# Fourier mixing and a gated feed-forward layer on one core: a row loaded 11 steps ahead, and a sigmoid written into PSUM

## The chip, the core and the metric

The kernel runs on one core of a Trainium2 chip. The metric is the device time of one execution in microseconds, as the median of several runs. The names of the engines are those of the profile: PE is TensorE's matmul, PEld its weight load, DVE is VectorE, ACT ScalarE, POOL GpSimd, and SP is SyncE, which here only issues transfers.

## The reference

The input x has 8 sequences of S = 3008 rows with 256 features. A Fourier transform runs over the rows and then over the features, and the real part is kept. Each row of the result then goes through a gated layer with 1536 hidden features, all in fp32:

```python
X = np.fft.fft(x, axis=1)
X = np.fft.fft(X, axis=2)
x = X.real.reshape(B * S, D)
gate = 1.0 / (1.0 + np.exp(-(x @ w_gate)))
val = x @ w_val
out = (gate * val) @ w_out
```

## The kernel before, in words

**Work.** The kernel uses the symmetry of a real transform. For one sequence it computes two tables, pk and qk, over k = 0 to 1504. Row k of the transform is their sum, and row S-k is their difference. So one pass over k gives the hidden features of two rows, k and S-k, and the matmuls are done once for both. The feature transform is merged into the gate and value weights ahead of the loop (G1 and G2).

**Loop.** A sequence is cut into 6 chunks of up to 252 values of k, and a chunk into 12 steps, one for each block of 128 hidden features. This makes 576 steps. A step i belongs to group p = i // 3. The profile calls the buffers of a step by name: pf is one PSUM bank with two halves, gate in `pf[:, 0]` and value in `pf[:, 1]`. Three banks take turns for pf. The helper `mm` at line 134 issues every matmul, so all of PE's rows carry L134, and the tile tells which they are.

The life of a step is spread over its neighbours:

- `seed(i)` (line 595, two ACT instructions, run in step i-1; none for the first 12 steps) fills the bank with row E, the contribution of the middle feature. E comes in a tile ek that one transfer broadcasts to 128 partitions for a whole chunk (line 583, in `e_rows`).
- `front_a(i)` (PE, pf<-pk) adds the pk part. `part(i)` (line 611, ACT) then copies twice the bank into the tile ae.
- `front_b(i)` (PE, pf<-qk) adds the qk part, after which the bank holds gate and value of rows k. It must come after the copy of line 611.
- `gate_a(i)`, in step i+1: ACT writes the sigmoid of the gate half to the tile h (line 630), and DVE subtracts the bank from ae into the tile z, gate and value of rows S-k (line 635; line 632 in a few early steps).
- `gate_b(i)`, in step i+1: DVE multiplies h by the value half of the bank (line 647), ACT takes the sigmoid of `z[:, 0]` (line 648), and DVE multiplies it by `z[:, 1]` into the other half of h (line 649). POOL then forms sums of blocks of h in the tile sf (line 655).
- `back(p, part)` (PE, po<-h,wf and po<-sf,wf, five matmuls in a step, ten records in the trace) multiplies by the output weights. This is a fast bilinear scheme, so at the end of each chunk DVE has 20 additions in the tile c (line 719) and some transposes and copies (lines 729 and 696) to do. They are put on a list, of which two or three are taken in each of the following steps.

**Order.** Every engine runs its instructions in the order written. In step i ACT runs line 630 for step i-1, 611 for i, 595 twice for i+1, and 648 for i-1; DVE runs 635, 647 and 649 for i-1 and then what it takes from the list. What is done beside the steps hangs on step numbers (`at(i, f)`): the mirrored copy of the next sequence in DRAM (lines 160 to 169), its load into x (line 148), folds of x on POOL (lines 388 to 417) and DVE (line 428), and the row E. The transfers of line 583 go through SP's queue, behind whatever SP was given before. Two buffers take turns for ek.

The whole transform of a later sequence (tiles ev and od) is computed in the midst of the steps, once per sequence.

Of the kernel before, what the change touches and what calls it, by code (L numbers as in the profile page):

```python
# [10 lines left out]
AF = mybir.ActivationFunctionType  # L11
ALU = mybir.AluOpType
# [69 lines left out]
def kernel(  # L82
# [10 lines left out]
    nc = tc.nc  # L93
# [35 lines left out]
    op = ctx.enter_context(tc.tile_pool(name="op", bufs=1))  # L129
# [440 lines left out]
    H, SF, EK = {}, {}, {}  # L570

    def cut(i):
        b, c, _ = groups[i // 3]
        k0, n = chunks[c]
        f = i % NFT
        return PQE[b], slice(k0, k0 + n), n, f, slice(f * P, (f + 1) * P)

    def e_rows(i):

        b, c, _ = groups[i // 3]  # L580
        k0, n = chunks[c]
        EK[i // NFT] = ekp.tile([P, CH], F32, name="ek", tag="ek")[:, 0:n]
        nc.sync.dma_start(out=EK[i // NFT], in_=ed[b : b + 1, k0 : k0 + n].to_broadcast([P, n]))

    PF, AP, Z = {}, {}, {}
# [51 lines left out]
    def block(p, i):  # L637

        R = 2 * chunks[groups[p][1]][1] // 3
        return H[p][:, i % 3, i // 3 * R : (i // 3 + 1) * R] if i < 9 else SF[p][:, i - 9, 0:R]  # L640

    def gate_b(i):

        n = cut(i)[2]
        p, fh = i // 3, i % 3
        z, h = Z.pop(i), H[p]
        nc.vector.tensor_tensor(h[:, fh, 0:n], h[:, fh, 0:n], PF.pop(i)[:, 1], op=ALU.mult)  # L647
        nc.scalar.activation(z[:, 0], z[:, 0], AF.Sigmoid)  # L648
        nc.vector.tensor_tensor(h[:, fh, n:], z[:, 0], z[:, 1], op=ALU.mult)  # L649
        if p < NG:  # L650
            return
        if fh == 1:
            SF[p] = sp.tile([P, 8, 2 * CH // 3], F32, name="sf", tag="sf")
        for dst, a, b, op in H_SUMS.get(fh, ()):
            nc.gpsimd.tensor_tensor(block(p, dst), block(p, a), block(p, b),  # L655
                                    op=(ALU.subtract, ALU.add)[op])
# [174 lines left out]
    def at(i, *fs):  # L831
        side.setdefault(i, []).extend(fs)
# [17 lines left out]
    i0 = NFT  # L850
# [12 lines left out]
    at(3 * i0 + 6, table_again)  # L863
    at(4 * i0 + 5, lambda: [at(4 * i0 + 6 + i, f) for i, f in enumerate(table_odd())])
    for i in range(i0, count, i0):
        at(i - 8, lambda i=i: e_rows(i))

    for b in range(B - 1):
        s0 = b * per
# [21 lines left out]
    for i in range(count):  # L891
        front_a(i)
        if N1 <= i < NFT:
            part(i)
        if i:
            gate_a(i - 1)
        if not N1 <= i < NFT:
            part(i)
        if i0 <= i + 1 < count:
            seed(i + 1)  # L900
        if i:
            gate_b(i - 1)
        for f in pre.pop(i, []) + use.pop(i, []):
            f()
        if i >= 5:
            back((i - 5) // 3, (i - 5) % 3)
        front_b(i)
        n = 3 if i >= count - 8 else 2 + i % 2
        for f in later[0:n]:
            f()  # L910
        del later[0:n]
        for f in side.pop(i, []):
            f()
    gate_a(count - 1)
    gate_b(count - 1)
    for f in later:
        f()
# [51 lines left out]
```

## Time and profile before

| | |
|---|---|
| Time, median of 3 runs | 1952.96 us (1952.14 to 1953.48) |
| The profiled execution's own time, and its span | 1955.09 us, 1953.3 us |
| Mean granted clock of TensorE | 0.995 |
| Busy: PE, PEld, DVE, ACT, POOL | 1919.4, 1781.1, 1587.8, 1330.9, 1611.4 us |
| Chain that ended last, by engine | PE 89%, DVE 4%, POOL 4%, ACT 1%, DMA 1% |
| Transfer ek<-ed (line 583) | 47 of them, 126 KB or 123 KB each |

The span is the time from the first to the last instruction. The chain that ended last is followed back from the last instruction, at each link to what released it. A wait "A <- B: 3.9, 7, 1.4" reads: A sat idle until B, 3.9 us in total, 7 times, 1.4 us the longest. In a timeline a row has its start, its length, the engine, line, operation, tiles and count, and in brackets the idle time before it and what ended it. Matmuls overlap each other in the record, so starts tell PE's pace better than lengths.

### The profile page before, as it was taken

The page shows a single profiled execution, that of the slowest core. Times are in us where ns is not written, and L with a number is a line of the kernel's source. Part 1 is how long each engine was busy: PE and PEld are TensorE (multiplying, and loading weights), DVE is VectorE, ACT ScalarE, POOL GpSimd, SP SyncE. Part 2 cuts the span into 40 slices and gives each one's busy share as a digit, 9 for nine tenths or more (in the row PEclk, how much of TensorE's full clock was granted, in tenths as well). Part 3 has the DMA queues.
Part 4 walks back from the last instruction along what each step waited for, and adds up shares of the span by engine and source line. Part 5 has one row for each costly group of instructions (what it writes and reads, how often), then busy time and mean ns, then how long its engine had stood idle before and what let it go on. Part 6 is the DMA issues. An engine that isn't in the chain of part 4 may idle for free.

```text
span 1953.3 us, 34335 instructions
## 1 busy us (share of the span) xinstructions
PE 1919.4 (98%) x11180; PEld 1781.1 (91%) x11180; DVE 1587.8 (81%) x3250; ACT 1330.9 (68%) x3120; POOL 1611.4 (82%) x2802
## 2 busy tenths in 40 slices
PE   6999999999999999999999999999999999999997
PEld 4779889999999999999999999999999999999997
DVE  6677898997888978888878887788788887777777
ACT  3566657666777677776777767777677766777775
POOL 3269998997999888997889979998799986777776
PEclk8999999999999999999999999999999999999999
DMA  8342413112012120212013121211210110011011
GB/s 270 104 129 16 115 36 103 46 24 83 14 47 57 16 79 14 57 49 78 15 25 79 17 79 25 47 49 21 83 17 14 22 20 14 14 22 19 15 19 27
DMA packets 171978, 96.78 MB, mean 50 GB/s; under 512 B 136090, under 2 KB 163868, under 8 KB 169252
## 3 DMA queue, kind: packets, MB, share of 16 engines
q1 hardware_dynamic: 169842, 94.06, 20.3%
q8 instruction: 90, 1.47, 0.3%
q10 hardware_dynamic: 1926, 0.52, 0.1%
q14 instruction: 88, 0.72, 0.1%
q0 software_dynamic: 32, 0.00, 0.0%
HBM read 69.83 MB, written 46.71 MB: 60 GB/s over the span
## 4 chain that ended last, share of the span: by engine, by line
PE 89%; DVE 4%; POOL 4%; ACT 1%; DMA 1%; SPq 0%; issue 0%; DVEq 0%; POOLq 0%; ACTq 0%
PE pf L134 46%; PE po L134 38%; PE ev L134 3%; POOL sf L655 2%; DVE c L719 2%; PE od L134 1%; DVE h L649 1%; PE ps L134 1%; DMA x<-in_xf_dram 1%; DVE z L635 1%; ACT z L648 1%; POOL x L401 0%; ACT pf L595 0%; DMA ek<-ed 0%; SPq L740 0%
## 5 line engine op out<-in xcount | busy, mean ns | idle before, releaser
L655 POOL TENSOR_TENSOR sf<-h 128x168 f32<-128x168 f32 (+1 forms) x940 | 539.7, 592 | 203.9 <-DVE h L649 203.8
L655 POOL TENSOR_TENSOR sf<-h,sf 128x168 f32<-128x168 f32 (+1 forms) x1128 | 645.1, 591 | 44.2 <-DVE h L649 44.2
L134 PE MATMUL pf<-qk,G 128*128 128x252 f32 (+1 forms) x2304 | 583.1, 376 | 4.0 <-ACT ae L611 3.9
L134 PE MATMUL pf<-pk,G 128*128 128x252 f32 (+1 forms) x2304 | 583.9, 376 | 2.3 <-ACT pf L595 2.3
L649 DVE TENSOR_TENSOR h<-z 128x252 f32<-128x252 f32 (+1 forms) x576 | 316.5, 549 | 301.3 <-ACT z L648 300.8
L595 ACT ACTIVATE pf<-ek,ge 128x252 f32<-128x252 f32 (+1 forms) x1128 | 531.6, 471 | 21.3 <-DMA ek<-ed 2.9
L134 PE MATMUL po<-sf,wf 128*128 128x168 f32 (+1 forms) x3008 | 519.8, 306 | 0.2
L719 DVE TENSOR_TENSOR c<-c 128x168 f32<-128x168 f32 (+1 forms) x929 | 505.7, 575 | 5.4 <-ACT c L696 0.3
L134 PEld LDWEIGHTS pf<-pk,G 128*128 128x128 f32 x2304 | 436.0, 190 | 56.4 <-ACT pf L595 3.4
L611 ACT ACTIVATE ae<-pf 128x504 f32<-128x504 f32 (+1 forms) x569 | 334.7, 588 | 217.3 <-PE pf L134 215.5
L134 PEld LDWEIGHTS po<-sf,wf 128*128 128x128 f32 x3008 | 463.4, 190 | 9.0 <-POOL sf L655 0.9
L134 PE MATMUL po<-h,wf 128*128 128x168 f32 (+2 forms) x2640 | 469.9, 307 | 0.0
L134 PEld LDWEIGHTS pf<-qk,G 128*128 128x128 f32 x2304 | 410.3, 190 | 37.6 <-ACT ae L611 6.7
L134 PEld LDWEIGHTS po<-h,wf 128*128 128x128 f32 x2640 | 420.7, 190 | 17.3 <-issue 0.9
L635 DVE TENSOR_TENSOR z<-ae,pf 128x504 f32<-128x504 f32 (+1 forms) x569 | 377.6, 664 | 16.2 <-ACT h L630 15.6
L648 ACT ACTIVATE z<-z 128x252 f32<-128x252 f32 (+1 forms) x576 | 232.7, 404 | 162.5 <-DVE z L635 147.5
L630 ACT ACTIVATE h<-pf 128x252 f32<-128x252 f32 (+1 forms) x576 | 216.4, 376 | 126.2 <-PE pf L134 118.9
L647 DVE TENSOR_TENSOR h<-h,pf 128x252 f32<-128x252 f32 (+1 forms) x576 | 232.1, 403 | 0.0
L655 POOL TENSOR_TENSOR sf<-sf 128x168 f32<-128x168 f32 (+1 forms) x188 | 108.6, 577 | 14.7
L655 POOL TENSOR_TENSOR sf<-sf,h 128x168 f32<-128x168 f32 (+1 forms) x188 | 106.8, 568 | 0.0
L134 PE MATMUL ev<-st,x 63*128 63x189 f32 (+3 forms) x372 | 73.6, 348 | 7.3 <-DVE x L398 7.1
L696 ACT COPY c<-po 128x504 f32<-128x504 f32 (+1 forms) x141 | 78.4, 556 | 3.1 <-PE po L134 3.1
(141 smaller groups left out, 898.9 us busy)
## 6 DMA issues: line engine op xcount, KB each, us to landing
x<-xr SPq DMA_DIRECT2D x14, 1536.0 KB
out_dram<-os SPq DMA_DIRECT2D x372, 56.0 KB
xr<-in_xf_dram SPq DMA_DIRECT2D x14, 768.0 KB
xr<-in_xf_dram SPq DMA_DIRECT2D x35, 256.0 KB
ek<-ed SPq DMA_DIRECT2D x39, 126.0 KB
out_dram<-os SPq DMA_DIRECT2D x284, 7.0 KB
st<-in_stab_dram SPq DMA_DIRECT2D x4, 1111.9 KB
x<-in_xf_dram SPq DMA_DIRECT2D x2, 1512.0 KB
```

Source lines behind the costliest of these rows:

```text
L134: nc.tensor.matmul(o, l, r, start=start, stop=stop, skip_group_check=True)
L595: nc.scalar.activation(PF[i][:, g], EK[i // NFT], AF.Copy, scale=ge[:, g, f : f + 1])
L611: nc.scalar.activation(AP[i], PF[i], AF.Copy, scale=2.0)
L630: nc.scalar.activation(H[p][:, fh, 0:n], PF[i][:, 0], AF.Sigmoid)
L635: nc.vector.tensor_tensor(z[:, :, ::-1], AP.pop(i), PF[i], op=ALU.subtract)
L647: nc.vector.tensor_tensor(h[:, fh, 0:n], h[:, fh, 0:n], PF.pop(i)[:, 1], op=ALU.mult)
L648: nc.scalar.activation(z[:, 0], z[:, 0], AF.Sigmoid)
L649: nc.vector.tensor_tensor(h[:, fh, n:], z[:, 0], z[:, 1], op=ALU.mult)
L655: nc.gpsimd.tensor_tensor(block(p, dst), block(p, a), block(p, b), op=(ALU.subtract, ALU.add)[op])
L696: (nc.vector.tensor_copy if t == 1 or t == 3 and not last else nc.scalar.copy)(C[0][:, 3 * t * R : 3 * (t + 1) * R], PO[t][:, 0 : 3 * R])
L719: engine.tensor_tensor(t[:, dst * R : (dst + 1) * R], *v, op=(ALU.subtract, ALU.add)[op])
```

## The change

Two edits that do not touch each other's lines.

The first is to `gate_b`. The bank of a step is kept until the end of it. The sigmoid of line 648 still reads `z[:, 0]`, but writes to `pf[:, 0]`, the gate half of the step's bank, which has been read by then. The multiply of line 649 reads it from there, so that one of its inputs lies in PSUM and one in SBUF. `z[:, 0]` is no longer written over.

The second is to the place of `e_rows`: the row E of a chunk is loaded 11 steps before the chunk's first step, where it was 8 steps. The first chunk that uses it (i = i0 = 12) keeps 8.

```diff
         p, fh = i // 3, i % 3
-        z, h = Z.pop(i), H[p]
-        nc.vector.tensor_tensor(h[:, fh, 0:n], h[:, fh, 0:n], PF.pop(i)[:, 1], op=ALU.mult)
-        nc.scalar.activation(z[:, 0], z[:, 0], AF.Sigmoid)
-        nc.vector.tensor_tensor(h[:, fh, n:], z[:, 0], z[:, 1], op=ALU.mult)
+        z, h, pf = Z.pop(i), H[p], PF.pop(i)
+        nc.vector.tensor_tensor(h[:, fh, 0:n], h[:, fh, 0:n], pf[:, 1], op=ALU.mult)
+        nc.scalar.activation(pf[:, 0], z[:, 0], AF.Sigmoid)
+        nc.vector.tensor_tensor(h[:, fh, n:], pf[:, 0], z[:, 1], op=ALU.mult)
...
     for i in range(i0, count, i0):
-        at(i - 8, lambda i=i: e_rows(i))
+        at(i - (8 if i == i0 else 11), lambda i=i: e_rows(i))
```

In the built program the number and order of the instructions on PE, DVE, ACT and POOL stay as they were. On SP the transfer of the second chunk's row now stands ahead of the two loads of x (line 148), and that of some later chunks ahead of a mirror transfer. Three kinds of waits are new targets of old instructions: the sigmoid of line 648 waits for the multiply of line 647 of its own step (before, for line 635), and the seed of line 595 and, in the first chunk, the first matmul into a bank wait for the multiply of line 649 of the step that had the bank (before, line 647).

## Prediction

> **What bounds the kernel now.** I asked four things in this order: is PE ever idle, who makes it wait, what does one such wait look like, and what do the touched instructions cost. First the table of busy time by stage (columns: stretch, its length, busy time of PE, PEld, DVE, ACT, POOL with counts, then clock and DMA):
>
> ```profile
> 140.00:150.00 10.00, 7.72 (x34) 6.78 (x34) 2.23 (x6) 3.88 (x10) 4.39 (x10) 0.83 0.44 40
> ...
> 160.00:320.00 160.00, 157.24 (x953) 143.53 (x953) 139.91 (x275) 104.38 (x251) 147.11 (x252) 1.00 0.27 69
> 320.00:480.00 160.00, 158.27 (x949) 146.90 (x949) 139.38 (x268) 106.81 (x256) 144.75 (x246) 1.00 0.22 56
> 480.00:800.00 320.00, 320.00 (x1901) 302.37 (x1900) 263.22 (x539) 228.88 (x534) 282.79 (x490) 1.00 0.18 41
> ```
>
> After 480 us PE is never idle, so nothing can be won there, only lost. What can be won lies in one hole near 144 us (2.28 us idle, and a clock of 0.83) and in 2.76 + 1.73 = 4.5 us of idle between 160 and 480 us. The waits name the causes:
>
> ```profile
> DVE h L649 <- ACT z L648: 300.8, 573, 4.3
> ...
> ACT z L648 <- DVE z L635: 147.5, 194, 2.9
> ...
> PE pf L134 <- ACT ae L611: 3.9, 7, 1.4
> ...
> PE pf L134 <- ACT pf L595: 2.3, 1, 2.3
> ```
>
> The last is the hole at 144 us, one event. The third is most of the 4.5 us. The second matters for the change: in 194 of 576 steps the sigmoid finds ACT idle because DVE was late; I call these late steps. The waits of two windows put 56 of them between 150 and 460 us and 131 between 460 and 1900 us.
>
> **The row E.** The hole in the timeline:
>
> ```profile
> 137.70 1.01 PE L134 MATMUL pf<-qk,G 128*128 128x252 f32 x4
> ...
> 137.83 1.89 SPq L583 DMA_DIRECT2D ek<-ed  x1
> ...
> 140.82 1.01 PE L134 MATMUL pf<-qk,G 128*128 128x252 f32 x4
> 143.08 0.98 ACT L595 ACTIVATE pf<-ek,ge 128x252 f32<-128x252 f32 x2 [2.89 <-DMA ek<-ed]
> 144.11 1.91 PE L134 MATMUL pf<-pk,G 128*128 128x252 f32 x4 [2.28 <-ACT pf L595]
> ...
> 148.17 1.01 PE L134 MATMUL pf<-qk,G 128*128 128x252 f32 x4
> ```
>
> Row E was issued at 137.83 us, behind a run of stores on SP, and landed just before 143.08, some 5.2 us later. A usual step lasts 140.82 - 137.70 = 3.12 us from qk to qk. This one lasts 148.17 - 140.82 = 7.35 us, so it loses 4.23 us: the idle time, and matmuls at half pace afterwards (four in 1.91 us, not 1.01). In the changed program the transfer stands ahead of the loads of x, which were issued at 118.32 us once the mirror copy had landed. Issued by then, it lands by some 118.3 + 5.2 = 123.5 us, and is wanted at 140.2 us, when ACT would have reached line 595. That is 16 us of cover, so I take the whole **-4.2 us**; if the transfer should still be late the term is 0, and nothing excludes that it is late by more. What it is moved past: the loads of x slip by its issue, at most 2.0 us in the rows of line 583, and the first fold of x on POOL is at 151.57 us, over 20 us after the traffic of these loads dies down; no cost. In later chunks the row passes a mirror transfer and stores on SP, and its buffer is free earlier than it is asked for; line 583 waited 7.6 us in 17 cases for the seeds, and behind it stand only stores and copies that are due later. No cost, and a row's length at most if that cover were gone.
>
> **The sigmoid in PSUM.** It removes and adds no instruction. Three prices change. The groups (busy, mean ns, idle before):
>
> ```profile
> L649 DVE TENSOR_TENSOR h<-z 128x252 f32<-128x252 f32 (+1 forms) x576 | 316.5, 549 | 301.3 <-ACT z L648 300.8
> ...
> L648 ACT ACTIVATE z<-z 128x252 f32<-128x252 f32 (+1 forms) x576 | 232.7, 404 | 162.5 <-DVE z L635 147.5
> ...
> L647 DVE TENSOR_TENSOR h<-h,pf 128x252 f32<-128x252 f32 (+1 forms) x576 | 232.1, 403 | 0.0
> ```
>
> *Gain: line 649.* With both inputs in SBUF it takes 415 to 1552 ns. It is 420 when POOL is idle, some 610 beside POOL's sums, more beside POOL's long folds. Line 647, of the same size with one input in PSUM, takes 390 to 414 ns whatever POOL does. I price the new 649 at 403 ns, 146 ns less on average: 576 x 0.146 = 84 us of DVE's busy time. This is no time of the kernel, since DVE is not the end of the chain after 480 us.
>
> *Price: the sigmoid's own length.* No row shows a sigmoid from SBUF to PSUM. The nearest are 404 ns (itself, SBUF to SBUF), 376 ns (line 630, PSUM to SBUF) and 472 ns (line 595, SBUF to PSUM, but with a scale taken from memory). I take 400 ns and keep 376 to 472. The Trainium skill, "ScalarE: Activation LUTs", section "What happens when an `exp` ACTIVATE runs", says that ScalarE reaches PSUM faster than SBUF; line 595, the slowest of the three rows, does not show it, and by the rule the price would lie below 404 ns, at an estimated 376, and the sum 1 us lower.
>
> *Price: the sigmoid's wait.* It now waits for line 647 instead of 635. This costs nothing where ACT was busy with line 595 until then, but in a late step it is on the path:
>
> ```profile
> 372.57 0.67 DVE L635 TENSOR_TENSOR z<-ae,pf 128x504 f32<-128x504 f32 x1
> 373.16 0.40 DVE L647 TENSOR_TENSOR h<-h,pf 128x252 f32<-128x252 f32 x1
> 373.27 0.41 ACT L648 ACTIVATE z<-z 128x252 f32<-128x252 f32 x1 [2.86 <-DVE z L635]
> ...
> 373.72 0.60 DVE L649 TENSOR_TENSOR h<-z 128x252 f32<-128x252 f32 x1 [0.15 <-ACT z L648]
> 373.85 0.58 ACT L611 ACTIVATE ae<-pf 128x504 f32<-128x504 f32 x1
> ...
> 374.24 1.26 DVE L719 TENSOR_TENSOR c<-c 128x168 f32<-128x168 f32 x2
> ...
> 374.49 1.12 PE L134 MATMUL pf<-qk,G 128*128 128x252 f32 x4 [1.02 <-ACT ae L611]
> ```
>
> Line 647 ends at 373.56, so the sigmoid would start at 373.58, **0.31 us later**. Behind it on ACT stand line 630 and the copy of line 611, for which PE waits here: this wait grows by 0.31 us. Line 649 starts 0.45 us after the sigmoid, at 374.03, and gives way 0.34 us after its start (what the 420 ns cases show) where it took 374.24 - 373.72 = 0.52. So line 719 starts at 374.37 instead of 374.24: a late step hands **+0.13 us** on to the next. Where 649 already took 420 ns it hands on +0.31; behind a long fold it hands on less than zero, and I count at most 0.4 us of that, for the next addition must wait for the same fold. Against it stands a relief that I can only bound: the additions of line 719 alternate with POOL's sums at 0.6 us each (1.26 for two), and 0.33 alone as at the end of the kernel; with 649 gone from the queue for POOL's port, the first of them may find the port free. That is 0 to 0.27 us per step.
>
> The late steps come in runs of about eight, and a run costs PE what it has handed on up to its last binding step, plus 0.31, less what PE had to spare there. I went through the runs with each step's own length of 649. Without relief the six runs of 150 to 450 us give +0.6, 0, +0.9, +0.2, +0.6 and +0.7 = 3 us. The one binding run in each of five later sequences, with 0.24 to 0.31 us to spare, gives +0.2. New restarts of PE cost 0.12 each, as its first matmuls after a wait show, some 15 of them: 3 + 5 x 0.2 + 1.8 = **+6 us**. With 0.15 us of relief per late step the runs come to -0.8 and no new restart is left. I take the middle in relief, 0.08, and as the sum is bent (few runs bind) **+2 us**. The ends: -4.5 us if all idle time of 160 to 480 us went, +10 us without relief and with 472 ns for the sigmoid (0.07 more, some 60 binding late steps).
>
> The Trainium skill speaks against this edit: "PSUM — Partial Sum Buffer", section "PSUM bank collisions raise a hardware error", has two engines kept apart by bank, not by address, so that sigmoid and multiply may not overlap although they touch different halves. The trace before holds no such pair; by the rule the wait of 0.31 us is needed and the sum stands, without it the edit could only win.
>
> **Priced at nothing.** The seed waits for 649 of the bank's last step; it started at least 0.74 us after the end of 647, and in the step above 649 would end at 374.44 and the seed start at 374.63. In the first chunk PE's next matmul into the bank came at 59.38 us and 649 ended at 58.35. The tail from 1942 us on is untouched.
>
> **Sum.** -4.2 + 2 = -2.2 us. On the profiled execution, 1955.09 us with a span of 1953.3, this makes 1952.9. That execution is 2.1 us above the median, so the forecast is 1952.96 - 2.2 = **1950.8 us**. A measurement of this kernel tells about 0.2%, 3.9 us, from no change.
>
> **Rivals.** *Relief (faster).* The freed port also shortens line 719 by 0.15 us or more per late step, runs no longer build up, and the idle time of 160 to 480 us shrinks: -4.2 - 0.8 to -4.2 - 4.5, so 1944.3 to 1948. For it speaks that 719 takes 700 ns between 360 and 450 us, against 0.33 alone; against it, POOL is busy for 90 to 92% of these windows and takes any port time that is left. *The sigmoid's wait wins (slower).* Each late step hands on 0.13 to 0.31 us with no relief, on 131 late steps after 460 us too, where PE had no idle time. It decides from the point where the runs cost over 8.1 us, which the sum without relief (+6) reaches with a sigmoid of some 440 ns: +3.9 to +6, or 1957 to 1959, and 1963 if runs that had 0.4 to 0.6 us to spare bind as well. *The row is still late.* No -4.2: 1955. The 16 us of cover speak against it.
>
> **Numbers.** Forecast 0.42, with its own range of 1948.5 to 1954.5; relief 0.30; the wait 0.23; the late row 0.05. Faster by over 0.2%: relief, and 0.03 of the forecast: 0.33. Slower: the wait, and 0.03 of the forecast: 0.26. Within: 0.36 + 0.05 = 0.41. The range leaves out the outer ends of relief and of the wait: 1946 to 1960 us.
>
> **What would show it.** Row: no wait of line 595 on ek near 140 us, and no dip of the clock there; the step from qk to qk is 3.1 us. Line 649: a mean near 405 ns. Wait: line 648 waits for line 647, and 649 for 648 by 0.45 us or so in late steps. Relief: the mean of line 719 and the idle time of PE from 160 to 480 us. I am wrong if PE is idle after 480 us for more than a few us, or if 649 stays above 450 ns.

## Result, and the profile after

The changed kernel takes 1945.14 us, the median of 15 runs, against 1951.93 us for the kernel before, also of 15 runs: 6.8 us faster by the medians. The ratio is 0.9964, with a 95% interval of 0.9954 to 0.9974, which makes 7.0 us (5.1 to 9.0). The forecast of 1950.8 us was 5.7 us too high, and the time lies just below the low end of the range (1946). The rival *Relief* (1944.3 to 1948) is what happened.

The profiled execution took 1944.18 us with a span of 1942.4 us. It lies 1 us below its median, the one of before 3 us above its own, so the two spans differ by 10.9 us, more than the kernels do. The chain that ended last is now 96% PE, where it was 89%, and POOL has gone from it.

The table of busy time by stage of the changed kernel (stretch, its length, busy time of PE, PEld, DVE, ACT, POOL with counts, clock, DMA):

```profile
140.00:150.00 10.00, 10.00 (x59) 9.39 (x58) 4.57 (x10) 7.15 (x17) 9.28 (x15) 1.00 0.54 19
160.00:320.00 160.00, 157.87 (x960) 144.82 (x959) 125.17 (x274) 106.73 (x255) 143.50 (x257) 1.00 0.31 76
320.00:480.00 160.00, 160.00 (x971) 150.57 (x970) 124.67 (x276) 110.45 (x262) 142.38 (x252) 1.00 0.21 52
480.00:800.00 320.00, 320.00 (x1903) 302.44 (x1903) 241.11 (x545) 227.15 (x533) 273.66 (x489) 1.00 0.18 42
```

The hole at 144 us and its dip of the clock are gone (10.00 of 10 busy, 7.72 before), 320 to 480 us is full (158.27 before), and after 480 us nothing is lost. DVE is busy 22 us less from 480 to 800 us, and that brings nothing there. The waits of the changed kernel:

```profile
DVE h L649 <- ACT pf L648: 427.7, 576, 1.2
...
ACT pf L648 <- DVE h L647: 103.2, 164, 3.1
...
PE pf L134 <- ACT ae L611: 2.0, 4, 0.9
```

The new wait of 648 for 647 is there, nearly as often as the old one for 635 (164 times, 194 before), and still PE's wait for the copy of line 611 fell from 3.9 us to 2.0. The wait of PE for line 595 has no row any more. The groups of the changed kernel (busy, mean ns, idle before):

```profile
L649 DVE TENSOR_TENSOR h<-pf,z 128x252 f32<-128x252 f32 (+1 forms) x576 | 241.6, 419 | 427.7 <-ACT pf L648 427.7
...
L719 DVE TENSOR_TENSOR c<-c 128x168 f32<-128x168 f32 (+1 forms) x929 | 438.5, 504 | 5.4 <-ACT c L696 0.2
...
L648 ACT ACTIVATE pf<-z 128x252 f32<-128x252 f32 (+1 forms) x576 | 214.4, 372 | 105.7 <-DVE h L647 103.2
```

And the additions of line 719 in the kernel before:

```profile
L719 DVE TENSOR_TENSOR c<-c 128x168 f32<-128x168 f32 (+1 forms) x929 | 505.7, 575 | 5.4 <-ACT c L696 0.3
```

Line 649 is 130 ns shorter (549 to 419), line 648 is 32 ns shorter (404 to 372), and line 719, which the change does not touch, is 71 ns shorter. Over 929 additions and 576 steps that is 0.12 us per step. This is the relief that the prediction could only bound. Nearly all of it falls on the addition that stands right behind line 649: the 321 additions in that place took 540 ns before and 367 now, the other 599 took 596 and 578.

**Where the time went.** Idle columns can understate a loss, since matmuls overlap each other in the record. I therefore compare when ACT starts the first seed (line 595) of a given step in each trace. The starts of the kernel before and the changed one are 100.38 and 98.88 us at step 12, 143.08 and 138.13 at step 24, 310.27 and 302.86 at step 72, 472.29 and 461.20 at step 120, and 1931.36 and 1920.26 at the last seed. The differences of these differences say where a kernel loses time against the changed kernel. The table has the kernels of the experiments below too, in us. Each row is one profiled execution, and some lie apart from their median (before 3.2 us above it, sig_649_first 3.6 us below), so a sum here need not be the difference of the medians:

```
                steps 12-24   24-72   72-120   120-last   sum
before              3.45       2.46     3.68     0.01     9.60
row_only            0.45       0.68     3.78     0.01     4.92
sig_only            3.80      -0.42     0.01     0.00     3.39
late_sigmoid        0.20       9.31    11.31    43.27    64.09
late_psum           0.00      -0.03     0.08     0.03     0.08
sig_649_first       0.39       0.33    -0.03    -0.01     0.68
even_list           0.00      -1.95     1.37     6.62     6.04
list_first          0.00      -2.81     1.54     0.02    -1.25
pool_writes         3.16      -3.29    -0.03     0.04    -0.12
row_9               0.00      -0.08     0.00     0.03    -0.05
```

The start-up ahead of step 12 is not in the sums: it differed by 1.5 us between the two first executions and is about as different between executions of one kernel (98.88 and 99.91 us for the changed one). The 3.45 us of before are mostly the hole (row_only, without it, has 0.45 there); what follows to step 120 is the sigmoid edit and the dip of the clock.

### The profile page after: what moved, and what is told of

It reads as the page before. It is cut to its first block, busy times and chain, and to the rows that moved or that the text cites. A ratio compares the mean times of both kernels' runs of the same rounds, so it can differ in the third digit from the quotient of the medians.

```text
span 1942.4 us, 34340 instructions
## 1 busy us (share of the span) xinstructions
PE 1913.1 (98%) x11180; PEld 1778.8 (92%) x11180; DVE 1445.2 (74%) x3250; ACT 1332.0 (69%) x3120; POOL 1565.7 (81%) x2802
## 4 chain that ended last, share of the span: by engine, by line
PE 96%; DVE 3%; DMA 1%; ACT 1%; issue 0%; SPq 0%; DVEq 0%
PE pf L134 49%; PE po L134 41%; PE ev L134 3%; PE od L134 1%; DVE c L719 1%; PE ps L134 1%; DMA x<-in_xf_dram 1%; DVE z L635 0%; ACT pf L648 0%; DVE h L649 0%; DVE h L647 0%; DVE os L729 0%; PE pe L134 0%; DVE x L428 0%; DVE x L392 0%
## 5 line engine op out<-in xcount | busy, mean ns | idle before, releaser
L655 POOL TENSOR_TENSOR sf<-h 128x168 f32<-128x168 f32 (+1 forms) x940 | 521.4, 574 | 225.6 <-DVE h L649 225.6
L655 POOL TENSOR_TENSOR sf<-h,sf 128x168 f32<-128x168 f32 (+1 forms) x1128 | 629.2, 578 | 59.1 <-DVE h L649 58.7
L649 DVE TENSOR_TENSOR h<-pf,z 128x252 f32<-128x252 f32 (+1 forms) x576 | 241.6, 419 | 427.7 <-ACT pf L648 427.7
L719 DVE TENSOR_TENSOR c<-c 128x168 f32<-128x168 f32 (+1 forms) x929 | 438.5, 504 | 5.4 <-ACT c L696 0.2
L648 ACT ACTIVATE pf<-z 128x252 f32<-128x252 f32 (+1 forms) x576 | 214.4, 372 | 105.7 <-DVE h L647 103.2
L655 POOL TENSOR_TENSOR sf<-sf,h 128x168 f32<-128x168 f32 (+1 forms) x188 | 102.9, 547 | 0.0
```

What stands on the lines that cost most here:

```text
L648: nc.scalar.activation(pf[:, 0], z[:, 0], AF.Sigmoid)
L649: nc.vector.tensor_tensor(h[:, fh, n:], pf[:, 0], z[:, 1], op=ALU.mult)
L719: engine.tensor_tensor(t[:, dst * R : (dst + 1) * R], *v, op=(ALU.subtract, ALU.add)[op])
```

## Experiments

Each edit is against the kernel named, each ratio against the kernel before, which was run beside all of them: 1951.88 us in the first group (row_only, sig_only, late_sigmoid, sig_649_first), 1951.29 in the second (late_psum, even_list, after_again, pool_writes), 1951.6 in the third (list_first, row_9).

**Each part alone.** row_only is the kernel before with the second edit alone:

```diff
-        at(i - 8, lambda i=i: e_rows(i))
+        at(i - (8 if i == i0 else 11), lambda i=i: e_rows(i))
```

> The row E is loaded 11 steps ahead; the sigmoid stays in SBUF as before. All theories agree on the mechanism: the hole near 144 us and the clock's dip after it are gone, 4.2 us by the steps of the trace before. Theory 'relief' (the sigmoid edit has a gain of its own, because line 649 leaves the port that DVE shares with POOL): 1947 to 1948 us beside a kernel before of 1952, so over half of the gain of 6.8 us, and 4 to 5 us of PE's idle time stay between 150 and 480 us. Theory 'row alone' (the sigmoid edit is worth nothing): the whole gain, 1945 us.

sig_only is the changed kernel with 8 steps again, so the first edit alone:

```diff
-        at(i - (8 if i == i0 else 11), lambda i=i: e_rows(i))
+        at(i - 8, lambda i=i: e_rows(i))
```

> The sigmoid goes to PSUM; the row stays 8 steps ahead. Theory 'relief': 2 to 4 us faster than before, so 1948 to 1950, the hole near 144 us as before, line 719 near 505 ns and line 649 near 420 ns. Theory 'row alone': 1952. My prediction's sum (the sigmoid's wait costs 2 us net): 1954.

Measured: row_only 1949.24 us, ratio 0.9987 (0.9977 to 0.9998), 2.6 us faster than before. sig_only 1948.82 us, ratio 0.9983 (0.9974 to 0.9991), 3.1 us faster. Together 5.7 us, against 6.8 for both in one kernel: the parts add up within their intervals. In the stages of row_only the hole is closed and the idle time of 160 to 480 us is as before:

```profile
140.00:150.00 10.00, 10.00 (x61) 9.46 (x59) 4.39 (x10) 7.03 (x18) 7.66 (x14) 1.00 0.45 25
160.00:320.00 160.00, 157.51 (x955) 144.14 (x954) 138.25 (x273) 105.34 (x252) 149.13 (x252) 1.00 0.29 71
320.00:480.00 160.00, 158.18 (x949) 146.82 (x948) 140.13 (x271) 106.08 (x253) 144.71 (x245) 1.00 0.21 56
```

In those of sig_only the hole is there, and 320 to 480 us is full:

```profile
140.00:150.00 10.00, 6.92 (x40) 6.21 (x40) 2.76 (x6) 5.00 (x12) 4.67 (x10) 1.00 0.51 40
...
320.00:480.00 160.00, 160.00 (x971) 150.58 (x970) 123.52 (x274) 110.92 (x263) 142.48 (x253) 1.00 0.23 57
```

So each edit does its own work in its own place. The clock column tells something more: with a hole of 3.08 us the granted clock stayed at 1.00 here, while the hole of 2.28 us in before came with a mean of 0.83. The price of the hole thus varies from one trace to the next.

**The wait without the freed port.** late_sigmoid is row_only with VectorE's multiply of rows k (line 647 in the kernel before) moved ahead of the subtraction, so that the sigmoid of rows S-k, still from SBUF to SBUF, starts one multiply later:

```diff
+        nc.vector.tensor_tensor(h[:, fh, 0:n], h[:, fh, 0:n], PF[i][:, 1], op=ALU.mult)
...
-        nc.vector.tensor_tensor(h[:, fh, 0:n], h[:, fh, 0:n], PF.pop(i)[:, 1], op=ALU.mult)
+        PF.pop(i)
```

> The row 11 steps ahead, sigmoid in SBUF as before, but DVE does the multiply by the value half ahead of the subtraction, so that the sigmoid of rows S-k starts a multiply later and DVE has 0.45 us and not 0.15 us to idle for it: the wait of the changed kernel without its port. Compared with the kernel that has the row alone. If the wait has the price of my prediction without relief: 5 to 6 us slower than the row alone, line 649 still near 550 ns, PE idle for 8 us or more between 150 and 480 us and for some us after it. If the wait is covered by PE's stock of work everywhere (the wait never mattered): within 1 us of the row alone.

Measured: 2010.29 us, ratio 1.0304 (1.0288 to 1.032), 61 us slower than row_only and far from what was expected. The new order has a wait of its own (the multiply needs the sigmoid of rows k first), so by itself this run does not say whether the delay or the order costs so much. late_psum settles that: the same order, but the sigmoid writes to PSUM, as in the changed kernel. Against late_sigmoid:

```diff
-        nc.scalar.activation(z[:, 0], z[:, 0], AF.Sigmoid)
-        nc.vector.tensor_tensor(h[:, fh, n:], z[:, 0], z[:, 1], op=ALU.mult)
+        nc.scalar.activation(pf[:, 0], z[:, 0], AF.Sigmoid)
+        nc.vector.tensor_tensor(h[:, fh, n:], pf[:, 0], z[:, 1], op=ALU.mult)
```

> Same order as in late_sigmoid (multiply of rows k ahead of the subtraction, so the sigmoid starts some 0.40 us later in late steps), but the sigmoid writes to PSUM and the multiply of rows S-k reads it there, as in the changed kernel. Against late_sigmoid only the place of the sigmoid's result differs. Theory (relief: the freed port pays for the wait): the multiply of rows S-k takes 419 ns, the additions of the list about 504 ns, PE waits for the copy of line 611 by some 2 to 4 us in all (32.1 us in late_sigmoid), time within 4 us of the changed kernel's 1945. Rival (it was the new order, with its wait for line 630 on VectorE, that cost the 61 us in late_sigmoid, not the missing relief): the multiply is short again but the time stays above 1980 and PE's wait for the copy above 15 us.

Measured: 1945.31 us, ratio 0.9964 (0.9952 to 0.9977), the time of the changed kernel. The groups of late_sigmoid (multiply of rows S-k, additions of the list, sigmoid) and PE's wait:

```profile
L721 DVE TENSOR_TENSOR c<-c 128x168 f32<-128x168 f32 (+1 forms) x929 | 490.8, 559 | 5.6 <-ACT c L698 0.5
...
L651 DVE TENSOR_TENSOR h<-z 128x252 f32<-128x252 f32 (+1 forms) x576 | 359.7, 624 | 346.0 <-ACT z L650 346.0
...
L650 ACT ACTIVATE z<-z 128x252 f32<-128x252 f32 (+1 forms) x576 | 235.3, 408 | 421.4 <-DVE z L637 407.1 <-DVE z L634 13.0
```

```profile
PE pf L134 <- ACT ae L611: 32.1, 55, 1.9
```

The same of late_psum:

```profile
L720 DVE TENSOR_TENSOR c<-c 128x168 f32<-128x168 f32 (+1 forms) x929 | 439.0, 504 | 5.4 <-ACT c L697 0.2
...
L650 DVE TENSOR_TENSOR h<-pf,z 128x252 f32<-128x252 f32 (+1 forms) x576 | 241.8, 420 | 427.0 <-ACT pf L649 427.0
...
L649 ACT ACTIVATE pf<-z 128x252 f32<-128x252 f32 (+1 forms) x576 | 214.4, 372 | 107.2 <-DVE z L637 91.5 <-DVE z L634 13.0
```

```profile
PE pf L134 <- ACT ae L611: 2.0, 4, 0.9
```

The two differ only in where the sigmoid's result lies, and in time by 65 us. With the result in SBUF the multiply takes 624 ns, the sigmoid is kept waiting 407 us in all, and PE loses time in every sequence whose steps carry a transform beside them (43 us after step 120). With the result in PSUM the delayed sigmoid costs nothing. So this is the answer to the wait: a later start of the sigmoid is dear where VectorE is slowed by GpSimd, and free where it is not. The sigmoid itself is 36 ns shorter too (408 to 372), against 204 ns of the multiply (624 to 420); the two were not separated.

**Who slows VectorE.** pool_writes is the kernel before with GpSimd's sums replaced by a memset of the same blocks:

```diff
-            nc.gpsimd.tensor_tensor(block(p, dst), block(p, a), block(p, b),
-                                    op=(ALU.subtract, ALU.add)[op])
+            nc.gpsimd.memset(block(p, dst), 0.0)
```

> The kernel before, with each sum of line 655 on GpSimd replaced by a memset of the same block: GpSimd writes SBUF as often, but reads nothing there; the output is not the reference's. Theory (line 649, with both inputs in SBUF, and the additions of line 719 share a path of reading with GpSimd's sums, and take turns with them): line 649 takes about 420 ns nearly everywhere, line 719 about 335 ns. Rival (any work of GpSimd in SBUF, or its instructions as such, slows them): both stay near 549 and 575 ns while GpSimd is busy.

Measured: 1944.36 us in one run, although this kernel still has the hole of before. Its groups:

```profile
L655 POOL MEMSET sf<- 128x168 f32 (+1 forms) x2444 | 462.7, 237 | 1143.8 <-PE po L134 1133.0
...
L718 DVE TENSOR_TENSOR c<-c 128x168 f32<-128x168 f32 (+1 forms) x929 | 284.8, 339 | 5.6 <-ACT c L695 0.5
...
L649 DVE TENSOR_TENSOR h<-z 128x252 f32<-128x252 f32 (+1 forms) x576 | 259.4, 450 | 576.2 <-ACT z L648 576.2
```

A memset is also shorter than a sum (237 ns against some 575), so the mean alone doesn't separate reading from being busy. The single instructions do: the 202 multiplies of line 649 that lay beside a memset took 420 ns on average, like the 311 beside nothing, while those beside the folds of lines 388, 398 and 401, which read, took 610, 817 and 697 ns. GpSimd's reading slows a VectorE instruction with two inputs in SBUF; its writing doesn't. Who starts first matters: five multiplies that began some 30 ns ahead of a fold of line 396 took 422 ns, and five that began 68 ns behind one of line 417 took 1208. The Trainium skill, "SBUF — State Buffer", section "Who interferes with whom", says just this: an instruction with two SBUF inputs contends with a GpSimd instruction that reads SBUF, not with one that only writes, and one with at most one SBUF input, outside the modes that use two ports, doesn't contend. The 419 ns of line 649 in the changed kernel, 419 to 421 beside sums and folds alike, agree. The runs show one thing more, that the addition right behind the relieved multiply gets shorter too.

**The wait taken away, the port left free.** sig_649_first is the changed kernel with the multiply of rows S-k ahead of the multiply of rows k, so that the sigmoid waits for line 635 again:

```diff
-        nc.vector.tensor_tensor(h[:, fh, 0:n], h[:, fh, 0:n], pf[:, 1], op=ALU.mult)
         nc.scalar.activation(pf[:, 0], z[:, 0], AF.Sigmoid)
         nc.vector.tensor_tensor(h[:, fh, n:], pf[:, 0], z[:, 1], op=ALU.mult)
+        nc.vector.tensor_tensor(h[:, fh, 0:n], h[:, fh, 0:n], pf[:, 1], op=ALU.mult)
```

> The changed kernel with the two multiplies of a step exchanged on DVE: the one that reads the sigmoid from PSUM goes first, the one by the value half second. The sigmoid then waits only for the subtraction, so it starts 0.31 us earlier in late steps, and ACT with it; DVE idles 0.45 us as in the changed kernel. If ACT's share of the wait is what is left of PE's idle time between 200 and 280 us: 1 to 3 us faster than the changed kernel, 1942 to 1944. If DVE's own work is what is late there: the same as the changed kernel within 1 us.

Measured: 1949.47 us, ratio 0.9985 (0.9973 to 0.9997), some 4 us slower than the changed kernel, not faster, with runs from 1945.92 to 1954.77. The profiled execution was the fastest of them, and there the sum against the changed kernel is only 0.68 us; so the cause of the 4 us is open. The five executions above 1952 us have a mean granted clock of 0.994 or 0.995, the seven below 1950 us one of 0.995 to 0.997, but there is no trace of a long one. The profile has one hint, the additions of the list:

```profile
L719 DVE TENSOR_TENSOR c<-c 128x168 f32<-128x168 f32 (+1 forms) x929 | 478.8, 546 | 5.1
```

They are longer (546 ns, not 504). What is shown is that even without the wait nothing is gained.

**What is left of the list.** even_list is the changed kernel with two items of the list in every step, and list_first the same in steps 36 to 71 only:

```diff
-        n = 3 if i >= count - 8 else 2 + i % 2
+        n = 3 if i >= count - 8 else 2
```

```diff
-        n = 3 if i >= count - 8 else 2 + i % 2
+        n = 3 if i >= count - 8 else 2 + (i % 2 if not 3 * i0 <= i < 6 * i0 else 0)
```

> The changed kernel, with two items taken from the list of additions in each step, where it was two and three in turn. Theory (what is left of PE's idle time in the steps comes from steps in which VectorE has three additions): fewer late steps, PE's wait for the copy of line 611 from 2.0 us to under 1 us, time 1 to 3 us below the changed kernel. Rival (the list is the same work and lasts longer into the next chunk, and the rest of the idle time has other causes, the turn of x at 250 to 273 us): within 1 us of the changed kernel, or some us slower if the list no longer empties in time for the next chunk's tile.

> The changed kernel, with two items of the list in each step of the chunks 4 to 6 (steps 36 to 71, some 175 to 300 us) alone, and two and three in turn elsewhere. In even_list these chunks took 1.95 us less than in the changed kernel, and each later sequence 1.40 us more, where the longer list met the folds of line 428. Theory (the idle time left in the changed kernel between 175 and 300 us comes from steps with three additions): 1 to 2 us less than the changed kernel, so 1943 to 1944, with the later sequences unchanged. Rival (the gain was a shift by the slow start of that execution): 1944.5 to 1946, and the seeds of chunk 7 as late as in the changed kernel.

> The changed kernel once more, beside the others on one chip and with its own profile: 1944 to 1946.5 us, line 649 at 419 ns, line 719 at 504 ns. It shows how much PE's waits for the copy of line 611 (2.0 us in the first profile) differ from one execution to the next.

Measured: even_list 1951.88 us, ratio 1.0001 (0.9992 to 1.001); list_first 1944.26 us, 0.996 (0.9946 to 0.9974); the changed kernel again 1945.07 us, 0.9962 (0.9949 to 0.9976), with lines 649 at 420 ns and 719 at 508 ns. even_list gains 1.95 us in steps 24 to 72, as expected, and loses 1.4 us in each later sequence, which the expectation for it had only as a rival. One such place in its timeline:

```profile
665.53 0.39 ACT L648 ACTIVATE pf<-z 128x252 f32<-128x252 f32 x1 [1.51 <-DVE h L647]
665.85 0.57 ACT L696 COPY c<-po 128x504 f32<-128x504 f32 x1
...
666.59 0.59 ACT L611 ACTIVATE ae<-pf 128x504 f32<-128x504 f32 x1
...
667.24 0.48 PE L134 MATMUL pf<-qk,G 128*128 128x252 f32 x1 [0.49 <-ACT ae L611]
```

The chain ahead of it goes through the list, the transposes of line 729 and the folds of line 428, one after the other on DVE: the longer list now lies beside the folds. list_first avoids the later loss, gains 2.81 us and gives 1.54 back within the next four chunks. Its 0.8 us below the changed kernel is no difference that 5 runs can tell.

**Why the row was late.** row_9 is the changed kernel with 9 steps in place of 11:

```diff
-        at(i - (8 if i == i0 else 11), lambda i=i: e_rows(i))
+        at(i - (8 if i == i0 else 9), lambda i=i: e_rows(i))
```

> The changed kernel with row E loaded 9 steps ahead, not 11. Theory (a place in SP's queue: what made the row late was the run of stores of the output that it was issued behind, and the loads of x around it): one step, 3.1 us, earlier than 137.83 us would be issued at some 134.7 if it still stood behind the stores, and land at 139.9 or so, just before it is wanted at 140.2, so no hole or one under 1 us. Rival (it is lateness by bandwidth: the transfer itself is slow beside the loads of x, 5 us from issue to landing or more): the row lands later than 141 us and a hole of over 1 us stays.

Measured: 1944.9 us in one run, and no hole. SP's timeline of row_9:

```profile
117.12 0.82 SPq L148 DMA_DIRECT2D x<-xr  x2
117.99 0.94 SPq L527 DMA_DIRECT2D x<-in_xf_dram  x1
118.97 8.61 SPq L583 DMA_DIRECT2D ek<-ed  x1
127.63 0.43 SPq L737 DMA_DIRECT2D out_dram<-os  x1
```

and of the changed kernel:

```profile
107.30 2.70 SPq L583 DMA_DIRECT2D ek<-ed  x1
116.36 0.82 SPq L148 DMA_DIRECT2D x<-xr  x2
117.23 0.94 SPq L527 DMA_DIRECT2D x<-in_xf_dram  x1
118.69 8.19 SPq L737 DMA_DIRECT2D out_dram<-os  x1
```

Neither expectation had the time of issue right. With 9 steps the row stands ahead of the stores: SP is held for 8.61 us at its issue, behind the loads of x, as it is held for 8.19 us at the first store in the changed kernel, and the seed that needs the row starts at 139.04 us without waiting for it. With 8 steps, in the kernel before, it stood behind 16 issues of stores and one more load of x, and was issued at 137.83:

```profile
121.03 7.68 SPq L737 DMA_DIRECT2D out_dram<-os  x1
...
136.92 0.87 SPq L527 DMA_DIRECT2D x<-in_xf_dram  x1
137.83 1.89 SPq L583 DMA_DIRECT2D ek<-ed  x1
```

So a single step of lead, past the stores, would have done; the place in SP's queue made the row late.

## Why the prediction was wrong, point by point

**Row E: right, at the upper edge of its price.** The prediction took -4.2 us. row_only measured -2.6 (interval -4.5 to -0.4), and the changed kernel stands 3.7 us below sig_only. The 4.2 us came from one execution with a dip of the clock; in sig_only, without a dip, the hole cost 3.35 us by step 36 (3.80 less 0.45 made up). The moved transfer cost nothing that shows: after step 24 row_only loses in no stretch over 0.1 us more than before.

**Line 649 and the sigmoid: right in kind.** 649 was put at 403 ns and took 419, whatever GpSimd did. The sigmoid was put at 400 ns with 376 as the rule's estimate; it took 372. Here the rule of the Trainium skill cited in the prediction, that ScalarE reaches PSUM faster than SBUF ("ScalarE: Activation LUTs", section "Step-by-step: what each stage is for"), agrees with the trace: 372 ns to PSUM, 404 to SBUF, from the same input. I had let line 595, which reads a scale from memory, speak against it.

**The wait: there, and priced right, but not decisive.** A late step of the changed kernel:

```profile
205.24 0.66 DVE L635 TENSOR_TENSOR z<-ae,pf 128x504 f32<-128x504 f32 x1
...
205.82 0.40 DVE L647 TENSOR_TENSOR h<-h,pf 128x252 f32<-128x252 f32 x1
206.25 0.38 ACT L648 ACTIVATE pf<-z 128x252 f32<-128x252 f32 x1 [2.23 <-DVE h L647]
...
206.67 0.42 DVE L649 TENSOR_TENSOR h<-pf,z 128x252 f32<-128x252 f32 x1 [0.45 <-ACT pf L648]
206.84 0.58 ACT L611 ACTIVATE ae<-pf 128x504 f32<-128x504 f32 x1
...
207.47 0.91 PE L134 MATMUL pf<-qk,G 128*128 128x252 f32 x3 [0.40 <-ACT ae L611]
```

It is the chain that the prediction drew: 648 behind 647, 649 behind 648, the copy of line 611 behind 648, and PE behind the copy. By the medians of the late steps the sigmoid starts 1.03 us after the start of line 635, 0.70 us before the change: 0.33 us of wait, forecast 0.31.

**The failed step: the relief, taken at 0.08 us and for late steps alone.** This term made +2 us of the sigmoid edit, where the runs give -3.1 (sig_only against before) to -4.1 (the changed kernel against row_only). It was wrong in two ways, which the groups between 150 and 460 us show. Of the kernel before:

```profile
L719 DVE TENSOR_TENSOR c<-c 128x168 f32<-128x168 f32 (+1 forms) x147 | 89.7, 640 | 0.8
...
L649 DVE TENSOR_TENSOR h<-z 128x252 f32<-128x252 f32 (+1 forms) x90 | 58.9, 654 | 35.4 <-ACT z L648 34.9
```

Of the changed kernel:

```profile
L719 DVE TENSOR_TENSOR c<-c 128x168 f32<-128x168 f32 (+1 forms) x157 | 82.9, 559 | 0.8
...
L649 DVE TENSOR_TENSOR h<-pf,z 128x252 f32<-128x252 f32 (+1 forms) x92 | 38.6, 420 | 59.8 <-ACT pf L648 59.8
```

First, its size. In the 56 late steps of before in this stretch there were 1.95 additions in a step. From the start of the first to the end of the last they took 635 ns each, and 548 ns each in the same steps of the changed kernel: 0.17 us of relief in a step. The prediction had bounded it at 0 to 0.27 us and then took 0.08; 0.15 us or more was the condition of *Relief*. The picture behind it was right: line 649 gone, the first addition of the step fell from 634 to 446 ns, and those after it stayed long (689 ns before, 685 now). With 649 down from 617 to 420 ns (0.20 us) and the sigmoid 0.03 us shorter, the terms give 0.31 - 0.20 - 0.03 - 0.17 = -0.09 us, where the prediction had 0.13 - 0.08 = +0.05. Measured in one piece, from the end of line 635 to the end of DVE's work for the step, these steps went from 2.88 to 2.83 us. That already turns the sign.

Second, its place. By the prediction's own sum, 0.15 us of relief in each late step makes the sigmoid edit worth some -0.8 us; the runs give more. 34 of the 90 steps of before are not late: the sigmoid finds ACT busy anyway, so the new wait costs nothing there. In these very steps line 649 was longest, 716 ns on average; 10 of them lay beside folds and took 1063. They now take 420 ns, and with 1.12 additions at 47 ns less each, such a step gives DVE 0.35 us (0.28 against row_only, where 649 took 659 ns in them). The prediction walked through the late steps and counted at most 0.4 us for what lay beside folds; it left out these steps. DVE then enters a run of late steps with less behind it, and the late steps, by the waits of the two windows, fell from 56 to 48 here and from 131 to 97 later. This second part is worked out from the traces and was not tried by itself; that the place of the sigmoid's result, and nothing else in the edit, pays for the wait is shown by late_sigmoid and late_psum.

**The +6 us "without relief" was not tried.** It took 649 as short while the additions stayed long, and the 1.8 us of new restarts in it did not come: PE's waits for the copy fell from 7 to 4. Where nothing is freed and the sigmoid is delayed, the price is 61 us, ten times as much, since then the losses come back in each sequence with a transform. That case wasn't the change's, but the sum would not have found it. No run has the case that the sum priced, 649 short and the additions long.

**The base and the range.** The forecast hung on 1952.96 us of three runs, and the larger samples give 1951.3 to 1951.9: 1 us of the miss. The range left out the outer end of *Relief*, although that rival had 0.30; there the time came to lie.

**Two engines on one bank.** The rule of the Trainium skill that the prediction held against the edit ("PSUM — Partial Sum Buffer", section "PSUM bank collisions raise a hardware error": two engines kept apart by bank) is kept in the built program, and the wait that it asks for is in the trace. A kernel in which sigmoid and multiply overlap in one bank wasn't tried.

## What to carry to other kernels

Where a VectorE instruction with two SBUF inputs lies beside GpSimd sums, moving one of its inputs to PSUM can pay for a wait that the move adds, because the instruction right behind it is relieved too. Price such an edit over all steps of a stretch, the ones in which the new wait is covered above all, and not only over those where it binds. And compare the same instruction's start in two traces to see where time is lost: idle time alone showed 2.2 us of the 4.9 that the sigmoid edit won between row_only and the changed kernel.

## What was unexpected of the hardware

- A hole of 2.28 us in PE's work came with a granted clock of 0.83 over ten microseconds in the trace of before, and one of 1.99 us with 0.83 in pool_writes (row below), while a hole of 3.08 us left it at 1.00 in sig_only. By step 36 the hole had cost 4.7 us in before (against row_only) and 3.35 us in sig_only, so a price taken from one execution can be off by a microsecond.

```profile
140.00:150.00 10.00, 8.01 (x36) 7.30 (x36) 2.78 (x7) 5.45 (x13) 2.87 (x6) 0.83 0.52 28
```

- GpSimd's memsets left VectorE's two-input multiply at 420 ns, while its folds, which read, stretched the same instruction to 610 to 817 ns.
- SP is held for some 8 us (7.68, 8.19, 8.61) at whatever it issues next after the loads of x, so the order of what stands there matters more than the number of steps.
